# Linear attention with decay and a token-mixing layer on one core: the receptance of the last batch loaded one token to a partition and turned by DMA transposes, two decay tables made in halves, and another order of all instructions

## The chip, the cores and the metric

The program runs on one of the eight cores of one Trainium2 chip. The metric is the device time of one execution in microseconds (us). A core has a matrix engine (TensorE, PE in the profile), a vector engine (VectorE, DVE), an engine for activation functions (ScalarE, ACT), a general engine (GpSimd, POOL) and a sequencer that only issues transfers (SyncE, SP). Each engine works through its own instructions in the order in which they were written, and waits on semaphores for the others. Transfers (DMA) are issued by SP, POOL or ACT and moved by sixteen DMA engines.

## The reference

There are 4 batches of 768 tokens, 8 heads of 48 channels. All arrays are in 32-bit floats.

```python
for t in range(S):                        # attention with a decaying state, per batch and head
    cur = einsum('bhd,bhe->bhde', u * k_t, v_t)
    y[:, :, t] = einsum('bhd,bhde->bhe', r_t, state + cur)
    state = w * state + einsum('bhd,bhe->bhde', k_t, v_t)
x = y.transpose(0, 2, 1, 3).reshape(B, S, 384)
theta = x @ w_theta                       # token mixing with a phase
yr = einsum('ts,bsd->btd', w_tok_r, x * cos(theta))
yi = einsum('ts,bsd->btd', w_tok_i, x * sin(theta))
u = x + yr + yi
out = u + maximum(u @ w_ch, 0)
```

## The kernel before

**The attention in chunks.** The tokens of a batch are cut into 6 chunks of 128, and the chunks are worked on in 3 pairs (`front`, one round of its loop for each batch and pair). In a chunk the factor w^(t-s) of a score is split: k is multiplied by w^-(t+1), the table `wpinv`, into `Kw`, and r by w^t into `Rw`, both with tokens on the partitions (L457). For the scores both are needed with channels on the partitions. So `flips` transposes eight blocks of 128x128 on TensorE (L416) into a bank of PSUM, and ACT or DVE copies the bank out (L206 and L207) into `KT` or `RT`. In the last batch (`turn_k`) `KT` is made by a DMA transpose from SP instead (`turned`, L425). The scores go to two banks (L487), DVE multiplies them by the mask of earlier tokens into `mAT` (L492), and then come the parts of the output: the diagonal term (`PD` on DVE L497, `dg`, then `yd` L512), the state's update (`Ta` and `St`, L539 to L547, copied to `Sb`), the state's share (L560) and the chunk's own share (L569). DVE adds them into `x` (L583).

**How r is laid out.** `load_r` brings a pair's 256 tokens with two neighbouring tokens in one partition (128 x 8 x 96 numbers, one issue of 384 KB). So the two halves of `Rw` hold the even and the odd tokens and take two tables, `wpow[:, 0]` and `wpow[:, 1]`; the copy out of PSUM puts the tokens back into order. k and v come one token to a partition, with one issue of 192 KB for each chunk (`load`).

**The mixing layer.** `x` is transposed to `xT` (in the last batch by DMA transposes). A matmul with `Wth` gives theta (L605), ACT takes sine and cosine into `sc` (L609), DVE multiplies by `x` into `z` (L612). `mixing` runs for each batch in two halves of 384 tokens: matmuls with the token weights `WrT` and `WiT` (L641), DVE adds `xT` into `uT` (L652), a transposed copy `un` of it is made, the channel matmul follows (L685), DVE finishes a tile into `fin` (L690) and SP stores it (L695). In batch 0 a mixing part is six matmuls of 128 columns. The token weights arrive through POOL's own transfers into six buffers `stg` (L395), are transposed on TensorE (L402) and copied out.

**What sets the order.** Each operation is a task with a number; `Plan` keeps what each one reads and writes. `ORDER` is a table of all tasks in the order in which they are written: `108P2` is task 108 on TensorE with its result in bank 2, and the letters P, V, A, G, S stand for TensorE, VectorE, ScalarE, GpSimd and SyncE. `emit` goes through the table; the letter says which engine runs the task, where more than one can. One more wait is added there: where DVE and POOL both run tasks that are marked as using their common port, a POOL task waits for the marked DVE task that was written last before it:

```python
            if t.port and letter == "V":
                last = ins
            elif t.port and letter == "G" and last is not None:
                tc.add_manual_dep(ins.ins, last.ins.name, SYNC, reason="shared port")
                last = None
```

Every load and store of batch data, and every DMA transpose, is issued by SP in the order of the table. What stands behind a transpose or a store on SP goes out only when that one's data is ready.

**The start.** ACT issues the load of w (`w_row`), TensorE spreads it over the partitions with one matmul (L274), ACT takes its logarithm (L314) and makes `wpinv` and the two tables `wpow` by exponentials (L319). `Wth` is loaded by POOL (L384), after a cast (L378) that holds it back until a load of batch 0 has landed; the first `stg` buffers are held back in the same way.

Of the kernel before, what the change touches and what calls it, by code (L numbers as in the profile page):

```python
# [16 lines left out]
F32 = mybir.dt.float32  # L17
# [11 lines left out]
6G 4G 8G 10G 16G 7G 11G 13G 1V 0A 27A 26A 21S 22S 23S 79S 78S 80S 3A 5V 12G 14V 29A 28A 128S 2P0 17A 18A 36G  # L29
9G 38V 40P1 19A 85G 20A 37V 39V 41A 42P2 43A 45P34 83V 87P5 48P67 88A 30A 31A 51V 84V 47V 46V 49V 86G 33G  # L30
89P0 52P1 90A 32A 134V 126S 24S 95P24 132V 25S 53V 98V 131V 137P5 99P3 92P60 82S 127S 81S 130S 129S 50V 96V
97V 100A 44A 55P1 138A 56V 64P3 174G 34G 35G 190G 212G 186G 178G 54G 182G 94V 59V 133V 60V 58A 57A 63P7 66P
67V 65V 187G 191G 179G 91A 135P2 102P4 68P5 136A 103V 104G 61A 69A 105A 62A 106A 143P01 74P7 93V 146V 101V
111P32 114P 112P 70P6 147P5 107V 144V 115V 113V 183G 170G 171G 108G 175G 148V 139A 76A 75A 71A 109A 150P4
151V 152G 154A 153A 72A 140P02 116P7 145V 117V 216S 188P3 192P5 142V 141V 110G 118P4 122P1 149G 189A 119A
193A 120A 77V 73V 124A 155P72 156P 158P 180P6 367P0 184P3 368P 185A 123A 159V 157V 181V 172P5 160P2 215S
214S 217S 261S 218S 262S 263S 265S 310S 264S 309S 206G 209G 200G 173A 360P4 361P 176P7 121V 203G 220G 161V
125V 222V 221V 219V 15G 162P6 166P3 353P1 177A 362P 354P 363P 355P 225P2 163A 164A 168A 167A 165V 169V 223P5
369P 370P 364P 226A 227A 224V 234V 231P76 232V 228P32 365P 356P 357P 238P5 366V 233V 239V 242V 266G 268G
235P7 371P 372P 241A 229V 267G 240G 270P4 373V 230V 376P6 358P 359V 236A 207P5 246P7 249P 247P3 210P0 378P2  # L40
374P1 271A 208V 403P4 201P5 377V 211A 202A 404P 405P 406P 407P 408P 204P6 311S 312S 313S 426S 473S 213G 197G
194G 375A 269V 237V 250V 248V 379A 205A 409V 316G 396P0 272P5 414P1 251P7 397P 398P 399P 400P 401P 243V 274G
273A 252A 244A 281V 285P2 275P34 278P65 314G 402V 282P7 286V 287G 245A 283A 288A 276V 290V 415A 280V 277V
# [100 lines left out]
def kernel(  # L144
# [13 lines left out]
    nc = tc.nc  # L158
    B, H, S, D = r.shape
    HD = H * D  # L160
    C = 128
# [16 lines left out]

    def turn_k(b):
        return b >= 3  # L180

    def turn_x(b):
        return b >= 3

# [8 lines left out]
    def bank(tok):  # L193
        return bank_t[P.bank_of[tok]]
# [546 lines left out]
```

## Time and profile before

| | |
|---|---|
| median of three runs | 136.80 us (136.79 to 137.02) |
| the profiled execution | 137.21 us |
| its span from first to last instruction | 135.5 us |
| PE busy in the span | 122.2 us |
| DVE busy | 114.2 us |
| ACT busy | 78.0 us |
| POOL busy | 68.8 us |
| granted clock of TensorE | 1.00 |

The profile shows one execution. Its span leaves out 1.7 us of its own 137.21 us, which lie before the first and behind the last instruction. The profile's views are: busy times of each engine; the chain of work that ended last, followed back from the last instruction; waits and what ended them; groups of equal instructions with their mean duration; the same busy times in chosen stretches of the span; and issues of transfers with the time until they landed. The trace has two rows for TensorE, matmuls (PE) and loads of stationary weights (PEld). A busy PE is not always a PE at full speed, since a matmul's end is modelled.

### The profile page before, as it was taken

Reading aid. Unit: us, or ns where it says so; the run is one execution under the profiler, and the core shown is the slowest. Engines: PE = TensorE matmul, PEld = TensorE weight load, DVE = VectorE, ACT = ScalarE, POOL = GpSimd, SP = SyncE. Lnnn points to the kernel's source line nnn. Section 1 sums busy time; section 2 is a strip of 40 time slices with the busy share of each in tenths; the row PEclk is TensorE's granted clock in tenths of the full one; section 3 lists DMA queues with packets and bytes.
Section 4 is the critical chain, followed back from the end, with each engine's and each line's share of the span. In section 5 each row is a group of like instructions: output and inputs, shape, how many; then the busy total and the mean of one; then the engine's idle time right before and its main releaser. Section 6 shows DMA issues by size and latency. Waiting matters only on the chain.

```text
span 135.5 us, 4188 instructions
## 1 busy us (share of the span) xinstructions
PE 122.2 (90%) x1667; PEld 91.9 (68%) x1667; DVE 114.2 (84%) x231; ACT 78.0 (58%) x145; POOL 68.8 (51%) x104
## 2 busy tenths in 40 slices
PE   3358778979999999999999999999999999999990
PEld 1136665858989987977766687776566676577950
DVE  5279989798999869998999999999999997575581
ACT  3665868798836779858387339799411337240020
POOL 7324477767658456548205999755249860000000
PEclk9999999999999999999999999999999999999999
DMA  4999999999998993399999977997989439734945
GB/s 78 225 252 203 192 186 258 222 217 190 238 211 198 192 188 63 137 204 237 244 193 229 254 139 200 151 202 148 223 220 203 97 69 112 171 119 174 92 171 177
DMA packets 79781, 24.65 MB, mean 182 GB/s; under 512 B 74257, under 2 KB 79762, under 8 KB 79762
## 3 DMA queue, kind: packets, MB, share of 16 engines
q1 hardware_dynamic: 76400, 21.44, 75.4%
q0 software_dynamic: 2528, 2.95, 13.1%
q8 instruction: 13, 0.21, 0.6%
q10 hardware_dynamic: 834, 0.00, 0.3%
q14 instruction: 6, 0.05, 0.1%
HBM read 20.06 MB, written 4.72 MB: 183 GB/s over the span
## 4 chain that ended last, share of the span: by engine, by line
PE 68%; DVE 14%; DMA 8%; issue 3%; ACT 2%; SPq 1%; POOL 1%; DVEq 0%; POOLq 0%
PE bank L641 31%; PE bank L416 11%; PE bank L685 7%; PE bank L605 5%; DMA stg<-in_moe_w_tok_r_dram 5%; PE bank L487 4%; DVE mAT L492 4%; DMA ld<-in_r_dram 4%; PE bank L525 3%; PE bank L569 2%; PE bank L402 2%; PE bank L560 2%; ACT RT L206 2%; DVE z L612 1%; DVE fin L690 1%
## 5 line engine op out<-in xcount | busy, mean ns | idle before, releaser
L641 PEld LDWEIGHTS <-z 128*128 128x128 bf16 x468 | 34.3, 98 | 11.1 <-DVE z L612 0.4
L641 PE MATMUL bank<-WrT,z 128*128 128x128 bf16 (+2 forms) x234 | 31.8, 264 | 0.2 <-DVE z L612 0.2
L641 PE MATMUL bank<-WiT,z 128*128 128x128 bf16 (+2 forms) x234 | 31.8, 264 | 0.0
L492 DVE TENSOR_TENSOR mAT<-bank,mask 128x512 bf16<-128x512 f32 x48 | 31.0, 679 | 0.2 <-PE bank L487 0.2
L457 POOL TENSOR_TENSOR Kw<-ld,wpinv 128x384 bf16<-128x384 f32 x17 | 17.1, 1012 | 14.5 <-DVE yd L512 5.4
L612 DVE TENSOR_TENSOR z<-sc,x 128x768 bf16<-128x768 bf16 x24 | 14.2, 604 | 2.5 <-ACT sc L609 2.5
L605 PE MATMUL bank<-Wth,xT 128*128 128x384 bf16 x72 | 15.5, 334 | 0.9 <-DVE xT L207 0.6
L609 ACT ACTIVATE sc<-bank,pi 128x384 bf16<-128x384 f32 x24 | 13.9, 588 | 4.2 <-PE bank L605 3.5
L206 ACT ACTIVATE Sb<-St 64x192 bf16<-64x192 f32 x29 | 10.3, 358 | 9.8 <-DVE St L547 3.7
L206 ACT ACTIVATE RT<-bank 128x1024 bf16<-128x1024 bf16 x12 | 12.3, 1027 | 6.1 <-PE bank L416 6.0
L652 DVE TENSOR_TENSOR uT<-bank,xT 128x384 bf16<-128x384 f32 (+1 forms) x25 | 13.0, 534 | 2.9 <-PE bank L641 2.7
L685 PE MATMUL bank<-Wch,uT 128*128 128x384 bf16 (+2 forms) x75 | 14.7, 319 | 0.0
L512 POOL TENSOR_TENSOR yd<-dg,vb 128x768 bf16<-128x768 f32 x9 | 13.3, 1475 | 0.7 <-ACT sc L609 0.6
L547 POOL TENSOR_TENSOR St<-Ta,wC 128x192 f32<-128x192 f32 x12 | 6.7, 556 | 13.4 <-DVE Ta L541 6.2
L583 DVE TENSOR_TENSOR x<-bank,yd 128x384 bf16<-128x384 f32 x24 | 12.3, 549 | 1.4 <-POOL yd L512 0.8
L457 POOL TENSOR_TENSOR Rw<-ld,wpow 128x384 bf16<-128x384 f32 x12 | 11.9, 1002 | 2.5 <-DVE Rw L457 2.3
L609 ACT ACTIVATE sc<-bank 128x384 bf16<-128x384 f32 x24 | 11.4, 494 | 1.8 <-PE bank L605 1.8
L690 DVE SCALAR_TENSOR_TENSOR fin<-bank,un 128x384 f32<-128x384 f32 x21 | 10.8, 548 | 0.9 <-DMA un<-uT 0.7
L487 PE MATMUL bank<-RT,KT 64*128 64x128 bf16 x192 | 9.2, 235 | 2.0 <-ACT RT L206 2.0
L206 ACT ACTIVATE un<-bank 128x384 bf16<-128x384 bf16 x8 | 3.7, 484 | 11.7 <-PE bank L416 11.7
L497 DVE TENSOR_TENSOR PD<-RT,KT 128x1024 bf16<-128x1024 bf16 x12 | 8.2, 686 | 2.0 <-ACT RT L206 1.9
L206 ACT ACTIVATE KT<-bank 128x1024 bf16<-128x1024 bf16 x7 | 7.1, 1021 | 4.2 <-PE bank L416 4.2
(81 smaller groups left out, 199.6 us busy)
## 6 DMA issues: line engine op xcount, KB each, us to landing
ld<-in_k_dram SPq DMA_DIRECT2D x24, 192.0 KB, 4.6
ld<-in_r_dram SPq DMA_DIRECT2D x12, 384.0 KB, 4.8
ld<-in_v_dram SPq DMA_DIRECT2D x24, 192.0 KB, 4.7
out_dram<-fin SPq DMA_DIRECT2D x21, 192.0 KB, 2.0
stg<-in_moe_w_tok_r_dram POOLq DMA_DIRECT2D x6, 192.0 KB, 5.6
stg<-in_moe_w_tok_i_dram POOLq DMA_DIRECT2D x6, 192.0 KB, 5.5
out_dram<-stg SPq DMA_DIRECT2D x2, 192.0 KB, 1.9
Wth<-in_moe_w_theta_dram POOLq DMA_DIRECT2D x1, 288.0 KB, 5.7
```

What stands on the lines that cost most here:

```text
L206: return nc.scalar.activation(o, i, Act.Copy)
L416: nc.tensor.matmul(bank16(tok)[:, i * C:(i + 1) * C], s, ident, is_transpose=True, start=(i == 0), stop=(i == n - 1))
L457: lambda e, c=c, src=src, tab=tab, dst=dst: eng_of[e].tensor_mul(dst[:, c, :, :D], src, tab.rearrange("p (h d) -> p h d", h=H)),
L487: nc.tensor.matmul(bank(tk[hi])[:, hp * C:(hp + 1) * C], KT[q, c, hp, :], RT[q, hp, c, :], start=(hp == 0), stop=(hp == HP - 1))
L492: P.add((DVE, dve_ns(HP * C)), lambda e, hi=hi, tk=tk, mAT=mAT: nc.vector.tensor_mul(mAT[:, hi], bank(tk[hi]).rearrange("p (h t) -> p h t" ...
L512: lambda e, yd=yd, dg=dg, vb=vb: eng_of[e].tensor_mul(yd.rearrange("p a h d -> p (a h) d"), wide(dg, D), vb.rearrange("p a h d -> p (a h) ...
L605: nc.tensor.matmul(bank(th)[:, :HD], xT[:, dk, to * C:(to + 1) * C], Wth[:, dk, :], start=(dk == 0), stop=(dk == ND - 1))
L609: P.add((ACT, act_ns(HD) - 5 + 95 * (1 - ri)), lambda e, th=th, sc=sc, ri=ri: nc.scalar.activation(sc[:, ri], bank(th)[:, :HD], Act.Sin, * ...
L612: P.add((DVE, dve_ns(2 * HD, 2.0)), lambda e, sc=sc, to=to: nc.vector.tensor_mul(z[:, to], sc, bc(x[:, to], 1, 2)), rd=[("x", xi, to), ("s ...
L641: nc.tensor.matmul(bank(tm)[:, q * n * C:(q + 1) * n * C], z[:, so, ri, dk * C:(dk + 1) * C], WT[:, so, w], start=(s0 == 0 and ri == 0 and ...
L652: nc.vector.tensor_add(uT[:, dks[0]:dks[-1] + 1, w0:w1], bank(tm)[:, :len(dks) * (w1 - w0)].rearrange("p (d t) -> p d t", d=len(dks)), xT[ ...
L685: nc.tensor.matmul(bank(tf)[:, :(d1 - d0) * C], uT[:, dk, j * C:(j + 1) * C], Wch[:, dk, d0 * C:d1 * C], start=(dk == 0), stop=(dk == ND - 1))
```

## The change

**The last batch's r.** A new switch `turn_r` is true for batch 3. There r is loaded like k, one token to a partition, with two issues of 192 KB in place of one of 384 KB. It is multiplied by a new table `wpnat` (w^t with t counted within the chunk), and `RT` is made by a DMA transpose from SP (`turned`), so that three times eight transposes on TensorE and three copies out of PSUM go.

**The decay tables.** The matmul that spreads w is cut into two of 192 columns, each with its own bank and its own logarithm; `wpinv` is made in two halves of columns. `wpow` stays in two whole tables, and `wpnat` is one more exponential on ACT.

**The order.** The whole table `ORDER` is another one. Batch 0 begins with r on SP and not with k. Many tasks that can run on two engines have another engine than before: on DVE there are 4 more copies of `KT`, 2 of `RT`, 3 more of `dg`, 1 more each of `WiT` and `un`, and one fewer each of `Rw`, `St`, `xT`, `yd` and the clearing of `Sb`, and two fewer of `WrT`. ACT has 13 tasks fewer. POOL has 5 more copies of `Sb`, the clearing of `Sb`, and one more each of `yd`, `St` and `Rw`. TensorE, apart from the transposes, does the same work.

```diff
 ORDER = """
-6G 4G 8G 10G 16G 7G 11G 13G 1V 0A 27A 26A 21S 22S 23S 79S 78S 80S 3A 5V 12G 14V 29A 28A 128S 2P0 17A 18A 36G
...
+14G 13G 10G 9G 11G 5G 17G 12G 15G 7G 8G 16G 1V 0A 30A 29A 26S 24S 25S 84S 83S 82S 130S 27S 28S 132S 131S 2P0
...
+    def turn_r(b):
+        return b >= 3
+
...
+    wpnat = sb.tile([C, HD], F32, name="wpnat")
...
-        P.add((PE, 1300), lambda e: nc.tensor.matmul(bank("w")[:, :HD], ones, w_row, start=True,
-                                                     stop=True),
-              rd=["w_row", "ones"], acq=["w"], prio=-100, mode=3)
+        halves = [slice(i * (HD // 2), (i + 1) * (HD // 2)) for i in range(2)]
+        for i, q in enumerate(halves):
+            P.add((PE, 650), lambda e, i=i, q=q: nc.tensor.matmul(
+                bank("w%d" % i)[:, q], ones, w_row[:, q], start=True, stop=True),
+                rd=["w_row", "ones"], acq=["w%d" % i], prio=-100, mode=3)
...
+        for i, q in enumerate(halves):
+            P.add((ACT, 290), lambda e, i=i, q=q: nc.scalar.activation(
+                lw_f[:, q], bank("w%d" % i)[:, q], Act.Ln), rd=["tab0"], use=["w%d" % i],
+                wr=[("lw_f", i)], prio=-97.9)
...
     def small_tables():
+        P.add((ACT, 520), lambda e: nc.scalar.activation(wpnat, lw_f, Act.Exp, scale=tok_f[:, 0:1]),
+              rd=[("lw_f", 0), ("lw_f", 1), "tok_f"], wr=["wpnat"], prio=-97.65)
...
-            ir = load_r(b, pr)
+            ir = load(b, pr, r) if turn_r(b) else load_r(b, pr)
...
+                        (Ls[ir].rearrange("p (c h d) -> p c h d", c=2, h=H)[:, c], wpnat, "wpnat", Rw, kR)
+                        if turn_r(b) else
                         (Ls[ir].rearrange("p (h c d) -> p c h d", c=2, h=H)[:, c], wpow[:, c],
                          ("wpow", c), Rw, kR)):
...
+            if turn_r(b):
+                flat = RT.rearrange("p h c t -> p (h c t)")
+                RT = flat.rearrange("p (c h t) -> p h c t", c=2, h=HP)
+                turned(flat.rearrange("p (a t) -> p a t", t=C), Rw.rearrange("p a h e -> p (a h e)"),
+                       pb, [kR, kR + (0,), kR + (1,)], [kRT], 1900)
+            else:
+                flips(RT.rearrange("p h c (t j) -> p h (c t) j", j=2),
```

The order is seen best at three places. In these rows a name is followed by the number of its buffer, and `x2` stands for two such rows in a run.

First DVE in the first 15 us, before. `ld` are buffers of loaded data, `PD` is the product of `RT` and `KT`, `dg` the small diagonal.

```order
L457 TENSOR_TENSOR Kw_97<-ld_85,wpinv 128x8x48
L457 TENSOR_TENSOR Rw_94<-ld_86,wpow 128x8x48 x2
L457 TENSOR_TENSOR Kw_98<-ld_88,wpinv 128x8x48
L497 TENSOR_TENSOR PD_113<-RT_106,KT_110 128x1024
L457 TENSOR_TENSOR Rw_95<-ld_89,wpow 128x8x48
L492 TENSOR_TENSOR mAT_116<-bank_65,mask_70 128x512
L492 TENSOR_TENSOR mAT_116<-bank_64,mask_70 128x512
L492 TENSOR_TENSOR mAT_117<-bank_67,mask_70 128x512
L457 TENSOR_TENSOR Rw_96<-ld_92,wpow 128x8x48 x2
L207 COPY dg_128<-bank_62 128x16
L497 TENSOR_TENSOR PD_114<-RT_107,KT_111 128x1024
L457 TENSOR_TENSOR Kw_99<-ld_91,wpinv 128x8x48
```

The same place on DVE in the changed kernel:

```order
L469 TENSOR_TENSOR Rw_95<-ld_87,wpow 128x8x48 x2
L469 TENSOR_TENSOR Kw_98<-ld_86,wpinv 128x8x48 x2
L210 COPY KT_111<-bank_64 128x1024
L469 TENSOR_TENSOR Rw_96<-ld_90,wpow 128x8x48
L515 TENSOR_TENSOR PD_114<-RT_107,KT_111 128x1024
L469 TENSOR_TENSOR Kw_99<-ld_89,wpinv 128x8x48
L510 TENSOR_TENSOR mAT_118<-bank_67,mask_70 128x512
L510 TENSOR_TENSOR mAT_117<-bank_66,mask_70 128x512
L510 TENSOR_TENSOR mAT_117<-bank_65,mask_70 128x512
L210 COPY RT_108<-bank_61 128x1024
L210 COPY KT_112<-bank_62 128x1024
L469 TENSOR_TENSOR Kw_100<-ld_92,wpinv 128x8x48
```

What moved: r's product stands ahead of k's, and three copies out of PSUM that ACT made (`KT` twice, `RT` once) now stand on DVE among the products.

Second POOL between 11 and 21 us, before. `stg` are the buffers of the token weights, the one-column casts hold a transfer back, and `uw` is a small product for the diagonal term.

```order
L457 TENSOR_TENSOR Rw_95<-ld_89,wpow 128x8x48
L333 TENSOR_TENSOR uw<-u_75,w_74 64x4 x2
L378 CAST stg_154<-ld_91 128x1
L378 CAST Wth<-ld_87 128x1
L384 DMA Wth<-in_moe_w_theta_dram 128x3x384
L378 CAST stg_158<-ld_91 128x1
L378 CAST Wch<-ld_91 128x1
L378 CAST stg_157<-ld_91 128x1
L378 CAST stg_155<-ld_91 128x1
L512 TENSOR_TENSOR yd_131<-dg_128,vb_101 128x768
L378 CAST stg_156<-ld_91 128x1
L395 DMA stg_157<-in_moe_w_tok_r_dram 128x768
```

The same place on POOL in the changed kernel:

```order
L405 DMA stg_156<-in_moe_w_tok_r_dram 128x768
L405 DMA stg_157<-in_moe_w_tok_i_dram 128x768
L388 CAST stg_154<-ld_92 128x1
L388 CAST stg_155<-ld_92 128x1
L388 CAST Wch<-ld_92 128x1
L469 TENSOR_TENSOR Kw_100<-ld_92,wpinv 128x8x48
L210 CAST Sb_127<-St_125 64x4x48
L343 TENSOR_TENSOR uw<-u_75,w_74 64x4 x2
L394 DMA Wth<-in_moe_w_theta_dram 128x3x384
L388 CAST stg_158<-ld_92 128x1
L530 TENSOR_TENSOR yd_132<-dg_129,vb_102 128x768
L565 TENSOR_TENSOR St_126<-Ta_124,wC 128x192
```

What moved: two transfers of token weights go out ahead of `Wth`, and `Wth` stands behind a copy `Sb`, which waits for the first state that DVE computes.

Third SP in the last batch, before. `in_k`, `in_r` and `in_v` are the inputs.

```order
L425 DMA_TRANSPOSE KT_110<-Kw_98 128x8x128
L353 DMA ld_85<-in_k_dram 128x8x48
L425 DMA_TRANSPOSE un_147<-uT_144 128x9x128
L353 DMA ld_85<-in_k_dram 128x8x48
L353 DMA ld_87<-in_v_dram 128x8x48 x2
L353 DMA ld_88<-in_k_dram 128x8x48 x2
L695 DMA out_dram<-fin_150 128x384
L425 DMA_TRANSPOSE KT_111<-Kw_99 128x8x128
L695 DMA out_dram<-fin_151 128x384
L695 DMA out_dram<-fin_152 128x384
L364 DMA ld_89<-in_r_dram 128x8x96
```

The same place on SP in the changed kernel:

```order
L435 DMA_TRANSPOSE KT_111<-Kw_99 128x8x128
L713 DMA out_dram<-fin_153 128x384
L713 DMA out_dram<-fin_151 128x384
L363 DMA ld_90<-in_r_dram 128x8x48
L435 DMA_TRANSPOSE RT_108<-Rw_95 128x8x128
L363 DMA ld_90<-in_r_dram 128x8x48
L363 DMA ld_89<-in_k_dram 128x8x48
L435 DMA_TRANSPOSE KT_112<-Kw_100 128x8x128
L363 DMA ld_91<-in_v_dram 128x8x48
L435 DMA_TRANSPOSE RT_109<-Rw_96 128x8x128
L363 DMA ld_91<-in_v_dram 128x8x48
L435 DMA_TRANSPOSE KT_113<-Kw_101 128x8x128
```

What moved: the three transposes of r stand between the transposes of k, the first of them behind two stores of batch 1, and the transpose `un` of batch 1 has gone further back.

More of the change, by code (lines that the diff above doesn't have):

```diff
@@ L34 @@
[L34 to L38, printed above, removed]
@@ L71 @@
+853V 813V 803P3 839P2 840P 841P 858P4 806P1 844P0 845P 846P 836P 847P 837P 842P 777S 780S 783S 801V 802S
+823V 804V 807V 848V 859A 838V 866P6 825P7 824S 805S 808S 843V 856P3 854P4 863P1 867V 826V 855V 857A 868S
+827S 864V 860P0 828P5 831P2 869P6 861V 829V 832V 870V 865S 862S 830S 833S 871S
 """
```

101 lines of the change are left out of this document (50 added, 51 removed).

## The prediction

> **What bounds the kernel now.** I read the page's head first, then the chain of work that ended last, then the busy times in stretches cut where the chain changes its engine, and last what DVE waited for. In the rows of the chain the columns are the start and the length in us.
>
> ```profile
> span 135.5 us, 4188 instructions
> 0.81 0.45 SPq L353
> 1.93 4.85 DMA ld<-in_r_dram
> 25.19 6.39 DMA stg<-in_moe_w_tok_r_dram
> 33.47 0.97 PE bank L605 x6
> 82.07 0.19 DVE x L583
> 98.23 0.43 PE bank L525 x16
> 130.74 0.50 PE bank L685 x3
> ```
>
> The chain starts with the load of r, goes through the front of batch 0 and a transfer of token weights, and reaches the last theta of batch 0 at 33.47 + 0.97 = 34.44. Behind that it is TensorE up to 82.07, DVE up to 98.23, then TensorE up to 131.24. So two engines share the bound. The stretches below are cut where DVE has finished the last `x` of batch 0 (31.2) and the last masked score `mAT` (111.5); the numbers behind the stretch's length are the busy times of PE, PEld, DVE, ACT and POOL.
>
> ```profile
> 0.00:10.00 10.00, 4.04 (x26) 2.30 (x26) 5.00 (x16) 5.45 (x7) 4.98 (x18) 1.00 0.84 182
> 0.00:31.20 31.20, 21.91 (x290) 16.45 (x290) 24.40 (x54) 21.75 (x38) 17.96 (x43) 1.00 1.03 204
> 31.20:111.50 80.30, 79.89 (x1207) 61.01 (x1205) 75.54 (x149) 50.59 (x96) 50.25 (x62) 1.00 0.91 184
> 82.00:98.00 16.00, 16.00 (x209) 10.95 (x207) 15.95 (x32) 13.43 (x26) 9.07 (x12) 1.00 1.03 192
> 111.50:135.50 24.00, 20.38 (x176) 14.44 (x174) 14.24 (x31) 5.68 (x12) 0.63 (x1) 1.00 0.68 145
> ```
>
> DVE is idle for 31.20 - 24.40 = 6.80 us in the first stretch, 5.00 of them in the first ten, and for 80.30 - 75.54 = 4.76 us in the second. Between 82 and 98 it is idle for 0.05. TensorE is idle for 0.4 in the second stretch. Whoever shortens one of the two alone gains little. What DVE waited for longest in the second stretch (sum in us, times, longest):
>
> ```profile
> DVE PD L497 <- ACT RT L206: 1.5, 2, 1.3
> DVE x L583 <- POOL yd L512: 0.8, 2, 0.5
> ```
>
> **The prices.** Groups of equal instructions: the last number before the second bar is the mean of one in ns. The rows under the dots are pieces of the chain, and then issues of transfers with KB and median us to landing.
>
> ```profile
> L207 DVE COPY KT<-bank 128x1024 bf16<-128x1024 bf16 x2 | 1.4, 692 | 0.2 <-PE bank L416 0.2
> L206 ACT ACTIVATE RT<-bank 128x1024 bf16<-128x1024 bf16 x12 | 12.3, 1027 | 6.1 <-PE bank L416 6.0
> L492 DVE TENSOR_TENSOR mAT<-bank,mask 128x512 bf16<-128x512 f32 x48 | 31.0, 679 | 0.2 <-PE bank L487 0.2
> L207 DVE COPY WrT<-bank 128x768 bf16<-128x768 bf16 x3 | 1.6, 550 | 0.2 <-PE bank L402 0.2
> L207 DVE COPY un<-bank 128x384 bf16<-128x384 bf16 x4 | 1.4, 348 | 0.9 <-PE bank L416 0.9
> L207 DVE COPY dg<-bank 128x16 f32<-128x16 f32 x3 | 0.5, 166 | 0.0
> L512 DVE TENSOR_TENSOR yd<-dg,vb 128x768 bf16<-128x768 f32 x3 | 3.1, 1048 | 0.0
> L547 DVE TENSOR_TENSOR St<-Ta,wC 128x192 f32<-128x192 f32 x4 | 1.4, 344 | 0.0
> L457 DVE TENSOR_TENSOR Rw<-ld,wpow 128x384 bf16<-128x384 f32 x12 | 7.3, 637 | 0.5 <-DMA ld<-in_r_dram 0.4
> L690 DVE SCALAR_TENSOR_TENSOR fin<-bank,un 128x384 f32<-128x384 f32 x21 | 10.8, 548 | 0.9 <-DMA un<-uT 0.7
> L305 DVE MEMSET Sb<- 128x960 uint32 x1 | 0.9, 858 | 0.1
> ...
> 33.14 0.34 PE bank L402 x6
> 41.64 0.34 PE bank L641 x6
> 54.95 0.49 PE bank L685 x3
> 80.49 0.45 PE bank L416 x8
> ...
> ld<-in_r_dram SPq DMA_DIRECT2D x12, 384.0 KB, 4.8
> ld<-in_k_dram SPq DMA_DIRECT2D x24, 192.0 KB, 4.6
> Wth<-in_moe_w_theta_dram POOLq DMA_DIRECT2D x1, 288.0 KB, 5.7
> KT<-Kw SPq DMA_TRANSPOSE x3, 4.1
> xT<-x SPq DMA_TRANSPOSE x6, 2.4
> ```
>
> The one price that no row has is a copy of `RT` on DVE. It cannot cost less than the equal copy of `KT` (0.69) and, at the rate of the slowest copy out of PSUM, `mAT` with 512 numbers in 0.679, not more than 1.36. I take 1.03, what ACT needs for it.
>
> Three rows from the timeline (start and length in us) are needed too. The first has the two tables for r, which end at 6.03, the second the last `x` of batch 0, which ends at 31.2, and the third a product of r on DVE that took 1.55 us against the mean of 0.64 while POOL multiplied at the same time.
>
> ```profile
> 4.92 1.11 ACT L319 ACTIVATE wpow<-lw_f,tok_f 128x384 f32<-128x384 f32 x2
> 30.17 1.02 DVE L583 TENSOR_TENSOR x<-bank,yd 128x384 bf16<-128x384 f32 x2
> 33.45 1.55 DVE L457 TENSOR_TENSOR Rw<-ld,wpow 128x384 bf16<-128x384 f32 x1
> ```
>
> **The change, part by part.** *The start, up to the last `x` of batch 0.* By the two orders DVE has three more copies of `KT` there (3 x 0.69 = 2.08), one of `RT` (1.03), two of token weights (2 x 0.55 = 1.10) and one more `yd` (1.05), and goes without one `St` (0.34), one `dg` (0.17) and one `xT` (0.55, a copy of the size of `WrT`): 5.26 - 1.06 = +4.2 us. The clearing of `Sb` (0.86) goes too, but it lay in the first ten us, where DVE is half idle, and so saves nothing. From the 4.2 comes what DVE can make up: at most the 6.80 - 5.00 = 1.8 us that it idles between 10 and 31.2, and at most 1.1 because r is now issued first (at 0.81 in place of 1.93, in the chain's first rows; but both loads of k are now behind it). So the shift lies between 1.3 and 4.2; I take 2.8, the middle. In this shift lies the later `Wth`: it now stands behind the copy of the first state on POOL and lands 5.7 us after its issue, but the theta that needs it is later by about the shift as well.
>
> *The second stretch, up to the last `mAT`.* DVE gets one `KT` (0.69), one `RT` (1.03), four `dg` (0.66), one `un` (0.35), and loses one `Rw` (0.64), three `WrT` (1.65), two `yd` (2.10) and three `fin` (1.64), which now stand behind it: 2.73 - 6.03 = -3.3 us. DVE's idle 4.76 us can shrink: ACT has 13 tasks fewer, and 1.5 us were waits for its `RT`. They can grow: POOL has five more copies of `Sb` and one more each of `yd`, `St` and `Rw`, and 0.8 us were waits for its `yd`; and three `PD` now wait for DMA transposes. Bounds -2 and +2; I take +0.3, a little on POOL's side, since a product on DVE beside one on POOL is slow (the row of 1.55 us).
>
> *Behind the last `mAT`* TensorE has two more channel tiles than before (2 x 0.49 = +1.0). The three more `fin` of DVE lie beside it, where DVE is busy for 14.24 of 24 us.
>
> The sum over DVE: 2.8 - 3.3 + 0.3 + 1.0 = +0.8 us.
>
> *The same over TensorE.* From the last theta of batch 0 on it starts 2.8 us later and has less to do: 24 transposes are gone (3 x 0.45 = 1.35), two token-weight blocks (0.68) and five mixing parts of batch 0 (1.70) stand ahead of that theta now: 2.8 - 3.73 = -0.9 us. That is 1.7 us earlier than DVE allows, so DVE's sum decides, and what was taken from TensorE becomes a wait for DVE.
>
> *Costed at nothing.* The halves of the tables: the tables' exponentials ended at 6.03 and r landed at 1.93 + 4.85 = 6.78, so the first products waited for loads; without that cover they are worth 0.4 at most. The extra exponential and ACT's 13 tasks: ACT idles 9.4 us in the first stretch. The split loads of r: two of 192 KB need about the time of one of 384 KB each (4.6 and 4.8), six issues on SP in place of three, early enough. The waits of SP: the first transpose of r stands behind two stores that need DVE's `fin` of batch 1; the scores that want it come some ten mixing parts later on TensorE (10 x 0.49), which is about what issue and landing take (4.1 plus half a us); if DVE is late there, scores and so `PD` are late.
>
> **The forecast.** The profiled execution's own time is 137.21 us, 1.7 more than its span and 0.4 above the median. The sum is a difference between two spans, and I carry it to the median unchanged: 136.8 + 0.8 = 137.6 us, slower. With the bounds of the shift and of the idle time narrowed to their middle halves it lies between 137.1 and 138.8.
>
> **Rivals.** *DVE catches up, and it is faster.* The place is DVE's idle time, 1.8 us in the start and 4.76 in the second stretch. If the shift is 2.0 and the idle time shrinks by 1.0 (most of the waits for ACT's `RT`), the sum over DVE is 2.0 - 3.3 - 1.0 + 1.0 = -1.3, TensorE's is 2.0 - 3.73 = -1.7, and the time is 135.5. At the best of both bounds TensorE decides with 1.3 - 3.73 = -2.4: 134.4. It turns where DVE makes up 1.1 us more than I gave it. For it speaks that ACT, which DVE waited for longest, has less to do; against it that DVE has no idle time between 82 and 98 to give.
>
> *Nothing to measure.* The two sums may meet between: 136.8. A difference within 0.2% of the time (0.27 us) is about what measurements of this kernel cannot tell from none.
>
> *The transposes of r come late.* A DMA transpose of eight blocks landed 4.1 us after issue, one of three blocks 2.4, so 0.8 a block; if eight cost eight times that, 6.4, each `RT` lands 2.3 later. TensorE's matmuls stand in a fixed order, so the first scores of the last batch wait for it once, and the later pairs' transposes queue behind one another on SP: 137.6 + 2 = 139.6. For it speaks that DMA engines are as busy as 1.03 and 0.91 of their time in the two long stretches, and that the transposes of k go through the same queue; against it the 4.1 itself, measured in that stretch.
>
> A rule speaks for this rival: the Trainium skill, page "VectorE: DVE Perf Modes", section "The three transpose paths", gives 1309 ns for a 128x128 block by DMA and 390 ns on TensorE, and advises TensorE where the result may go to PSUM. By it eight blocks would take 10.5 us (an estimate) and the time would be above 141. The trace does not agree for eight blocks in one transfer: 4.1 us.
>
> **How the numbers follow.** The forecast gets 0.40, the faster rival 0.35, no difference 0.10, late transposes 0.15. So faster has 0.35, same 0.10, slower 0.40 + 0.15 = 0.55. The range runs from 135.2, which leaves out the best fifth of the faster case, to 139.2, which leaves out the worst half of the late transposes.
>
> **What would show it.** Right: the last `x` of batch 0 ends near 34, 2 to 4 us later than 31.2; TensorE shows waits for DVE in the middle; DVE is over 96% busy from there to its last `mAT`, which ends near 111.3, and TensorE ends about 20.9 us behind it. Wrong: an early end of that stretch (before 109.5) means that DVE caught up; scores that wait for `RT<-Rw` mean late transposes; a copy of `RT` on DVE near 0.7 or 1.3 moves the sum by 0.6 down or up; and a start that ends before 33 makes it faster.

## The result, and the profile after

The changed kernel takes 138.15 us (median, 137.75 to 139.24), the kernel before beside it on the same chip 136.80 (136.59 to 137.02). The ratio is 1.0107, with a 95% interval of 1.0066 to 1.0148: slower, as forecast. The forecast was 137.6 us with a range from 135.2 to 139.2. The profiled execution took 138.46 us. Its span of 136.7 us stands against 135.5 before, 1.2 more. The ratios here and below leave out executions more than 1.5% above the fastest of their kernel; the profile of turn_late shows one of these, so it has no landmarks in the table below.

The page's head, and pieces of the chain of work that ended last (start and length in us):

```profile
span 136.7 us, 4146 instructions
18.74 5.89 DMA Wth<-in_moe_w_theta_dram
24.77 1.12 PE bank L623 x3
35.80 1.34 PE bank L659 x24
94.15 2.44 PE bank L659 x15
100.90 1.44 POOL yd L530
102.84 0.47 DVE x L601
103.32 4.64 DMA RT<-Rw
108.00 0.62 PE bank L505 x16
114.10 4.02 DMA xT<-x
130.73 0.50 PE bank L703 x3
```

Before, the chain ran through r's load and a load of token weights to the last theta of batch 0. Now it reaches the first theta (L623, at 24.77) through the load of `Wth`. From about 30 to 100 nearly all long pieces are TensorE's. In the last batch a transfer of `RT`, another of `xT`, and POOL's `yd` are on it, which were not there before.

The same stretches as before, cut at the end of the last `x` of batch 0 (35.03) and of the last `mAT` (111.3); behind the length stand the busy times of PE, PEld, DVE, ACT and POOL:

```profile
0.00:10.00 10.00, 5.07 (x40) 3.72 (x40) 5.26 (x19) 5.37 (x9) 6.69 (x18) 1.00 0.91 187
0.00:35.03 35.03, 25.61 (x330) 19.97 (x331) 26.90 (x57) 21.16 (x39) 22.62 (x50) 1.00 1.07 206
35.03:111.30 76.27, 76.00 (x1140) 57.12 (x1137) 72.34 (x148) 42.70 (x82) 52.16 (x63) 1.00 0.86 181
111.30:136.70 25.40, 21.32 (x181) 14.83 (x179) 15.51 (x33) 5.85 (x13) 0.00 (x0) 1.00 0.67 176
```

Against the prediction's rows the start is 35.03 - 31.20 = 3.8 us longer, the second stretch 80.30 - 76.27 = 4.0 shorter, and what lies behind the last `mAT` 25.40 - 24.00 = 1.4 longer: +1.2 in all. DVE's busy time grew by 26.90 - 24.40 = 2.5 us in the start and fell by 75.54 - 72.34 = 3.2 in the second stretch. Its idle time grew from 6.80 to 8.13 and fell from 4.76 to 3.93. TensorE stands still for 0.27 us of the second stretch.

Prices that the prediction had to estimate (groups and issues), and waits that are new or longer (sum in us, times, longest):

```profile
L210 DVE COPY RT<-bank 128x1024 bf16<-128x1024 bf16 x2 | 2.4, 1224 | 0.3 <-PE bank L426 0.2
RT<-Rw SPq DMA_TRANSPOSE x3, 4.0
PE bank L623 <- DMA Wth<-in_moe_w_theta_dram: 0.9, 1, 0.9
PE bank L505 <- DMA RT<-Rw: 0.2, 1, 0.2
DVE WrT L210 <- PE bank L412: 1.1, 1, 1.1
DVE Ta L559 <- PE bank L543: 1.0, 1, 1.0
DVE x L601 <- POOL Rw L469: 0.9, 1, 0.9
```

### The profile page after: what moved, and what is told of

Same layout as the page of the kernel before. It is cut to its first block, busy times and chain, and to the rows that moved or that the text cites. A ratio compares the mean times of both kernels' runs of the same rounds, so it can differ in the third digit from the quotient of the medians.

```text
span 136.7 us, 4146 instructions
## 1 busy us (share of the span) xinstructions
PE 122.9 (90%) x1645; PEld 91.9 (67%) x1645; DVE 114.8 (84%) x235; ACT 69.7 (51%) x132; POOL 74.8 (55%) x113
## 4 chain that ended last, share of the span: by engine, by line
PE 66%; DMA 11%; DVE 7%; POOL 7%; ACT 3%; issue 3%; DVEq 0%; SPq 0%; POOLq 0%; ACTq 0%
PE bank L659 29%; PE bank L426 10%; PE bank L623 9%; PE bank L703 5%; DMA Wth<-in_moe_w_theta_dram 4%; DMA RT<-Rw 3%; PE bank L505 3%; DMA xT<-x 3%; ACT sc L627 3%; PE bank L587 3%; PE bank L578 2%; PE bank L543 2%; PE bank L412 2%; POOL Rw L469 1%; DVE Rw L469 1%
## 5 line engine op out<-in xcount | busy, mean ns | idle before, releaser
L659 PEld LDWEIGHTS <-z 128*128 128x128 bf16 x468 | 34.3, 98 | 11.0 <-issue 0.7
L659 PE MATMUL bank<-WiT,z 128*128 128x128 bf16 (+2 forms) x234 | 31.2, 264 | 0.0
L530 POOL TENSOR_TENSOR yd<-dg,vb 128x768 bf16<-128x768 f32 x10 | 14.8, 1476 | 4.2 <-DVE z L630 2.7
L623 PE MATMUL bank<-Wth,xT 128*128 128x384 bf16 x72 | 15.5, 340 | 1.6 <-DMA Wth<-in_moe_w_theta_dram 0.9
L627 ACT ACTIVATE sc<-bank,pi 128x384 bf16<-128x384 f32 x24 | 13.3, 580 | 6.3 <-PE bank L623 6.1
L630 DVE TENSOR_TENSOR z<-sc,x 128x768 bf16<-128x768 bf16 x24 | 13.0, 567 | 3.2 <-ACT sc L627 3.1
L209 ACT ACTIVATE Sb<-St 64x192 bf16<-64x192 f32 x24 | 8.6, 359 | 7.8 <-DVE St L557 4.8
L469 POOL TENSOR_TENSOR Rw<-ld,wpow 128x384 bf16<-128x384 f32 x8 | 7.9, 995 | 8.5 <-DVE Kw L469 2.7
L209 ACT ACTIVATE vb<-ld 128x768 bf16<-128x768 f32 x10 | 8.4, 840 | 5.8 <-DMA ld<-in_v_dram 5.8
L426 PE MATMUL bank<-ident,Rw 128*128 128x128 bf16 x72 | 7.1, 248 | 3.6 <-POOL ident masks.py:199 1.8
L209 ACT ACTIVATE RT<-bank 128x1024 bf16<-128x1024 bf16 x7 | 7.2, 1026 | 5.3 <-PE bank L426 5.1
L623 PEld LDWEIGHTS <-xT 128*128 128x128 bf16 x72 | 6.1, 99 | 5.2 <-ACT Sb L209 1.0
```

Source lines behind the costliest of these rows:

```text
L209: return nc.scalar.activation(o, i, Act.Copy)
L426: nc.tensor.matmul(bank16(tok)[:, i * C:(i + 1) * C], s, ident, is_transpose=True, start=(i == 0), stop=(i == n - 1))
L469: lambda e, c=c, src=src, tab=tab, dst=dst: eng_of[e].tensor_mul(dst[:, c, :, :D], src, tab.rearrange("p (h d) -> p h d", h=H)),
L530: lambda e, yd=yd, dg=dg, vb=vb: eng_of[e].tensor_mul(yd.rearrange("p a h d -> p (a h) d"), wide(dg, D), vb.rearrange("p a h d -> p (a h) ...
L623: nc.tensor.matmul(bank(th)[:, :HD], xT[:, dk, to * C:(to + 1) * C], Wth[:, dk, :], start=(dk == 0), stop=(dk == ND - 1))
L627: P.add((ACT, act_ns(HD) - 5 + 95 * (1 - ri)), lambda e, th=th, sc=sc, ri=ri: nc.scalar.activation(sc[:, ri], bank(th)[:, :HD], Act.Sin, * ...
```

## The experiments

Four theories are told apart. P is the prediction: DVE's sum decides. T says that from about 33 us on TensorE's own queue decides, so that only its waits count, above all those for `Wth` and for `RT`. H came from the traces: TensorE works at half rate in the start, and the changed order puts off its full rate. C, which came last, is a chain in the last batch through POOL and SP. The expectations compare with the changed kernel's 138.15 us or its ratio.

All runs with their landmarks, from the same three cuts of each profile (us):

| run | ratio to before, 95% interval | first theta starts | last `x` of batch 0 ends | last `mAT` ends | span |
|---|---|---|---|---|---|
| before | 1 | 22.4 | 31.2 | 111.5 | 135.5 |
| changed | 1.0107 (1.0066 to 1.0148) | 24.8 | 35.0 | 111.3 | 136.7 |
| after_again | 1.0084 (1.0053 to 1.0115) | 24.8 | 35.1 | 111.0 | 136.1 |
| wth_early | 1.0230 (1.0193 to 1.0266) | 26.5 | 36.3 | 112.5 | 137.6 |
| copies_act | 1.0269 (1.0240 to 1.0298) | 27.2 | 37.2 | 113.1 | 138.2 |
| spin_gap | 1.0106 (1.0067 to 1.0145) | 24.9 | 34.4 | 110.8 | 136.2 |
| spin_after | 1.0108 (1.0067 to 1.0149) | 25.0 | 34.3 | 111.3 | 136.5 |
| spin_before | 1.0006 (0.9976 to 1.0036) | 24.3 | 32.5 | 112.5 | 136.3 |
| rw_early | 1.0204 (1.0161 to 1.0247) | 24.8 | 35.1 | 112.3 | 137.4 |
| rw_first | 1.0156 (1.0124 to 1.0189) | 24.4 | 34.2 | 111.7 | 136.8 |
| rw_dve | 1.0112 (1.0058 to 1.0165) | 24.2 | 34.3 | 111.0 | 136.3 |
| r_on_pe | 1.0475 (1.0443 to 1.0507) | 24.7 | 35.1 | 115.6 | 141.0 |
| turn_before | 1.0667 (1.0632 to 1.0703) | 22.5 | 31.3 | 120.4 | 144.3 |
| turn_late | 1.0938 (1.0889 to 1.0987) | - | - | - | - |

The landmarks of a row are those of one profiled execution, the ratio is of all. The profiled execution of spin_before took 138.03 us, against a median of 136.83. And rw_early, rw_first, rw_dve and r_on_pe change only the last batch, so that their start is that of the changed kernel. The last `x` of batch 0 ends between 34.2 and 35.1 in these profiles, so differences of up to 0.9 us at this mark arise without an edit there.

Two columns can be read before any experiment is told. From the last `mAT` to the end of the span it is 25.0 to 25.5 us in every run of the changed order, and 23.8 to 24.0 in every run of the order before. And a later start arrives at the last `mAT` nearly in full: wth_early +1.3 and +1.2, copies_act +2.1 and +1.8.

**The start: the load of `Wth`.**

```diff
 ORDER
-194G 38G 182G 183G 187G ... 37G 39G 190G
+194G 38G 39G 182G 183G 187G ... 37G 190G
```

> The changed kernel with one move: POOL issues the load of Wth right behind the cast that holds it back, ahead of the copy of the first state and of five other casts. In the changed kernel it was issued at 18.74 and TensorE waited 0.9 us for it at the first theta. Theory P (the prediction: DVE's sum decides, the later Wth lies inside DVE's shift): no difference to the changed kernel, 138.1 us, 1.0 to 1.4 above the kernel before. Theory T (TensorE's own queue decides from about 33 us on, and the wait for Wth is one of the places where it lost what the missing transposes gave): 0.5 to 0.9 less than the changed kernel, about 137.4, and the first theta starts near 23.5 in place of 24.77.

It became slower, 139.7 us, which neither theory expected. TensorE no longer waits for `Wth`, but for the first token weights, which now load behind it, and longer:

```profile
PE bank L411 <- DMA stg<-in_moe_w_tok_r_dram: 2.8, 1, 2.8
0.00:36.26 36.26, 24.85 (x330) 19.45 (x331) 26.05 (x57) 21.07 (x39) 22.30 (x50) 0.91 1.07 205
```

The DMA engines are taken for 1.07 of the time in this start as in the changed kernel's, so a transfer put ahead pushes another back. TensorE's matmuls stand in a fixed order, and in the changed order the flips of token weights stand ahead of the first theta. Moving these flips as well, the other half of this experiment, wasn't tried.

**The start: DVE's copies.**

```diff
 ORDER
-45V ... 92V ... 94V ... 140V
+45A ... 92A ... 94A ... 140A
```

> The changed kernel with four copies in the start given back to ACT: the three KT and the one RT of batch 0 that it had put on DVE. DVE has 3 x 0.69 + 1.2 = 3.3 us less work before the last x of batch 0, ACT four copies of 1.03 more. Theory P (DVE's load in the start is what made it slower): the last x of batch 0 ends 1.3 to 2.8 earlier than 35.0 and the time falls until TensorE's sum decides, 1.0 to 1.7 less than the changed kernel: 136.4 to 137.1. Theory T (TensorE decides and only waits for the first copies to be ready): a copy takes 1.03 on ACT and 0.69 on DVE, so the scores of batch 0 start later, 0 to 1.5 us more than the changed kernel: 138.1 to 139.6.

It became slower by more than any theory expected: 140.1 us, where T ended at 139.6 and P forecast a gain. This is the run against the prediction's way of sizing the start:

```profile
0.00:37.16 37.16, 25.88 (x330) 20.38 (x331) 24.51 (x53) 24.17 (x43) 22.02 (x50) 1.00 1.05 200
37.16:113.07 75.91, 75.63 (x1140) 57.09 (x1137) 72.33 (x147) 42.97 (x82) 52.07 (x63) 1.00 0.90 180
PE bank L504 <- ACT RT L208: 2.0, 1, 2.0
PE bank L504 <- ACT KT L208: 1.1, 1, 1.1
```

DVE has 26.90 - 24.51 = 2.4 us less to do, and the start is 2.1 us longer. The scores wait for the copies on ACT instead. How long the start takes is here not set by DVE's sum, but by how soon each piece is ready.

**The start: TensorE's rate.** Six transposes of `x` took 0.85 us at 22.45 and 0.51 at 28.54 in the changed kernel. By the gaps between matmuls the full rate comes at 24.4 us in the kernel before, at 27.3 in the changed kernel's first profile and at 28.7 in that of after_again. The following runs fill TensorE's gaps with matmuls that nobody reads: spin_gap the one ahead of the first theta, spin_after (whose edit is shown) and spin_before nearly all of the start, so that it works almost without a break.

```diff
+    wfill = sb.tile([C, C], BF16, name="wfill")
...
+    for i, n in enumerate([17, 8, 3, 24, 14, 8, 9, 5, 5, 18, 9, 13, 4, 4, 5, 5, 4, 6, 20, 6, 4, 11]):
+        def spin(e, i=i, n=n):
+            for _ in range(n):
+                nc.tensor.matmul(bank(("spin", i))[:, :C], wfill, wfill, start=True, stop=True)
+        P.add((PE, 56 * n), spin, rd=["wfill"], acq=[("spin", i)])
```

> The changed kernel once more, beside the kernel before on this chip, so that the three others stand against it. All theories: 1.0 to 2.0% above the kernel before (first measured: 1.0107 with 1.0066 to 1.0148).

The changed kernel once more: 138.05 us, 1.0084.

> The changed kernel with eight matmuls of 128 columns that nobody reads, put on TensorE ahead of the first theta, where it waited for Wth from 23.85 to 24.77 (8 x 0.107 = 0.86 us at the rate of that stretch). Theory H (half rate: TensorE takes 1.03 us for eight transposes until 27.3 us and 0.45 from then on, in the kernel before until 24.4; it goes to the full rate only after a stretch of unbroken work, and the wait for Wth broke it; a microsecond at half rate costs 0.47): the full rate comes between 23 and 26, and the time is 0.5 to 1.5 us less than the changed kernel's on the same chip. Theory T (the waits themselves are the cost, not the rate): no difference, since the wait is only filled. Theory P (DVE's sum): no difference.

> The changed kernel with 202 matmuls of 128 columns that nobody reads, put on TensorE into the gaps from 3.7 to 30.5 us (17 ahead of the first transposes of r, then 3 to 24 in each gap). Theory H (TensorE runs at half rate until it has worked for a stretch without a break): the full rate comes near 8 to 12 in place of 27.3, eight transposes of batch 0 take 0.45 in place of 1.03, and the time is 1.5 to 3 us less than the changed kernel's on the same chip, below the kernel before. Theories T and P: the matmuls only stand in the way of real work: no gain, 0 to 2 us more.

> The same for the kernel before: 204 matmuls of 128 columns that nobody reads, in the gaps of TensorE from 3.4 to 30.2 us. Theory H: the full rate comes near 8 to 12 in place of 24.4, and the time is 0.7 to 2 us less than the kernel before. Against the changed kernel with the same filling: if the later full rate was what took back the 24 transposes (1.35 us) in the start, the changed kernel is now the faster by about 0.4 us, 1.35 less the 0.95 us that it waits in the last batch. Theories T and P: no gain, 0 to 2 us more, and the changed kernel stays 1.0 to 1.5 us behind.

The filling did to the rate what it should. In spin_gap the first theta already runs at the full rate, its three matmuls in 0.65 us, and yet the time is the changed kernel's (1.0106). Eight transposes of `Kw`, in the changed kernel and in spin_after:

```profile
12.20 1.03 PE L426 MATMUL bank<-ident,Kw 128*128 128x128 bf16 x8 [0.35 <-POOL Kw L469]
```

```profile
12.57 0.61 PE L428 MATMUL bank<-ident,Kw 128*128 128x128 bf16 x8
0.00:34.34 34.34, 31.51 (x532) 28.03 (x533) 26.24 (x58) 21.06 (x39) 22.53 (x50) 1.00 1.08 208
34.34:111.26 76.92, 76.38 (x1140) 57.12 (x1137) 72.44 (x148) 42.45 (x82) 52.08 (x63) 1.00 0.89 179
```

TensorE is at its full rate 17 us earlier, and the time is that of the changed kernel: 1.0108 against 1.0084 and 1.0107. The last `x` of batch 0 ends 0.7 us earlier than in the changed kernel, and the second stretch takes that much longer. The kernel before with the same filling is at 1.0006, so the changed kernel stays as far behind as without it.

For those 0.7 us no filling is needed. In rw_first and rw_dve, whose start is the changed kernel's, the first theta (at 24.44 and 24.24) runs at the full rate as well. The first row is the changed kernel's, the second rw_first's:

```profile
24.77 1.12 PE L623 MATMUL bank<-Wth,xT 128*128 128x384 bf16 x3 [0.92 <-DMA Wth<-in_moe_w_theta_dram]
24.44 0.65 PE L622 MATMUL bank<-Wth,xT 128*128 128x384 bf16 x3 [0.66 <-DMA Wth<-in_moe_w_theta_dram]
```

Their last `x` of batch 0 ends at 34.2 and 34.3. In after_again, rw_early and r_on_pe, where the first theta takes 1.12 us, it ends at 35.1. So when the full rate comes differs between executions of one order, and a late one goes with 0.7 to 0.9 us at this mark. Of that little or nothing is left at the last `mAT`: 110.8 in spin_gap and 111.3 in spin_after, against 111.3 and 111.0. Theory H falls as the cause of the longer time.

**The last batch: the late `RT`.** On POOL the last product of r ended at 103.3, its transpose landed at 107.96, and TensorE's scores started at 108.00. Three runs move that product.

```diff
 ORDER, rw_early
-645G 725G
+725G 645G
 ORDER, rw_first
-698G 724G 722G 723G 644A 645G 725G ... 726S 727S
+723G 725G 698G 724G 722G 644A 645G ... 727S 726S
 ORDER, rw_dve
-793V ... 698G 724G 722G 723G 644A 645G 725G
+698G 724G 722G 723G 725V 793V ... 644A 645G
```

> The changed kernel with one move: on POOL the last product of r (second half of the last pair) goes ahead of the yd of the last batch's first pair. It then ends near 101.9 in place of 103.3, and the third DMA transpose of r can be issued and land 1.4 us earlier, near 106.6 in place of 107.96. Theory P (DVE's sum decides): yd is 1.0 us later, DVE's x behind it too, so 0 to 1.0 us more than the changed kernel: 138.1 to 139.1. Theory T (TensorE decides, and the third late RT starts three waits of TensorE with 0.94 us in sum, at 108.0, 118.2 and 119.9): 0.5 to 0.9 less than the changed kernel, about 137.4.

> The changed kernel with both products of r of the last pair moved on POOL ahead of a state update and the two products of k, into time in which POOL waited (94.9 to 97.5), and the third DMA transpose of r ahead of that of k on SP. yd keeps its place. RT should land near 103 in place of 107.96, KT near 106. Theory T: the three waits of TensorE in the last batch (0.94 us in sum in the changed kernel's profile) go: 0.5 to 0.9 us less than the changed kernel (1.0084 to 1.0107 of the kernel before), that is 1.002 to 1.006. Theory P (DVE's sum decides): no difference to the changed kernel. If the state update, later by 0.5 us, is what x waits for, it is slower.

> The changed kernel with the last product of r moved from POOL to DVE, ahead of four additions to uT at 99.9 us; POOL's other products keep their order. RT of the last pair can be issued near 101.5 and land near 105.7 in place of 107.96, yd keeps its place on POOL or is a little earlier, and DVE has one product more (0.55 us) ahead of x. Theory C (in the last batch a chain through POOL and SP decides: products of r, then yd, and the transpose of r behind them; what was moved on POOL alone only put yd in the place of RT): 0.4 to 0.9 us less than the changed kernel, that is 1.003 to 1.008 of the kernel before. Theory P (DVE decides): 0.3 to 0.6 us more than the changed kernel, 1.011 to 1.014.

In rw_early `yd` comes a microsecond later and DVE's `x`, which stands ahead of `PD` and the masks on DVE, waits for it. In rw_first it is the same, since the product went into POOL's queue ahead of `yd` all the same. The first row is rw_early's, the second rw_first's:

```profile
DVE x L600 <- POOL yd L529: 1.4, 2, 1.2
35.12:112.25 77.13, 76.52 (x1140) 56.98 (x1137) 73.00 (x148) 42.56 (x82) 51.89 (x63) 1.00 0.87 176
```

```profile
DVE x L600 <- POOL yd L529: 1.4, 2, 1.2
34.17:111.67 77.50, 76.79 (x1144) 57.24 (x1141) 73.48 (x147) 42.67 (x81) 51.76 (x63) 1.00 0.87 179
```

The second stretch is 0.9 and 1.2 us longer than the changed kernel's 76.27; rw_first's start ended 0.9 earlier, so that at its last `mAT` 0.4 is left of the 1.2. Only rw_dve moves the product without delaying `yd`. There the transpose goes out at 100.89 in place of 103.32, and TensorE shows no wait for `RT` any more:

```profile
100.89 1.25 SPq L434 DMA_TRANSPOSE RT<-Rw  x1
34.29:111.00 76.71, 76.51 (x1146) 57.33 (x1143) 72.88 (x148) 42.58 (x82) 51.51 (x62) 1.00 0.88 180
111.00:136.30 25.30, 21.41 (x181) 14.81 (x179) 15.51 (x33) 5.88 (x13) 0.00 (x0) 0.99 0.65 172
```

The time is 1.0112, the changed kernel's. The last `mAT` ends at 111.0, as in after_again. DVE works from 97 to 111 with masks, r's product, additions to `uT`, `x`, `PD` and masks, and once more `x`, `PD` and masks, idle for 0.5 us of it, and an `RT` that is there earlier finds it busy:

```profile
97.00:111.00 14.00, 13.92 (x182) 8.91 (x180) 13.54 (x26) 2.01 (x7) 10.58 (x13) 1.00 0.65 135
```

TensorE is as full: 13.92 us here, 13.77 in the changed kernel. The scores that need the third `RT` start at 107.44 in place of 108.00, but in after_again, the same kernel as the changed one, they start at 107.66. So the late transpose is seen on TensorE, and removing its wait gives no gain in the profile. T's and C's forecast (C: 1.003 to 1.008) isn't borne out, though the interval, 1.0058 to 1.0165, does not exclude its upper end. Nor can P's rise of 0.3 to 0.6 us be told from none, with 1.0112 against 1.0107 and 1.0084.

**The turning on TensorE again.**

```diff
-                turned(flat.rearrange("p (a t) -> p a t", t=C), Rw.rearrange("p a h e -> p (a h e)"),
-                       pb, [kR, kR + (0,), kR + (1,)], [kRT], 1900)
+                flips(flat.rearrange("p (a t) -> p a t", t=C),
+                      [Rw[:, c, 2 * hp:2 * hp + 2, :] for c in range(2) for hp in range(HP)],
+                      ("TR", b, pr), pb, [kR, kR + (0,), kR + (1,)], [kRT])
```

> The changed kernel with the last batch's r still loaded one token to a partition, but turned on TensorE (24 transposes of 128x128, three copies out of PSUM on ACT) and not by DMA. Theory P (DVE decides, TensorE has 1.7 us to spare): no difference to the changed kernel, 138.1 us. Theory T (TensorE decides; the DMA transposes saved it 24 x 0.056 = 1.35 us and cost it 0.94 us of waits in the last batch): 0.4 more than the changed kernel, about 138.5. If the late transposes cost more than they save, it is faster than the changed kernel: below 137.7.

It is 3.7% behind the changed kernel, more than any theory had, because of where the flips went. The third flips got a bank that DVE's masks still read, and a copy of `RT` on ACT stood ahead of the `dg` that `yd` waits for:

```profile
PE bank L425 <- DVE mAT L510: 1.5, 1, 1.5
PE bank L543 <- ACT dg L208: 0.6, 1, 0.6
35.06:115.64 80.58, 77.79 (x1164) 58.26 (x1161) 72.41 (x148) 45.24 (x85) 52.14 (x63) 1.00 0.80 159
```

TensorE's work in the stretch grew by 1.8 us (76.00 to 77.79), its idle time by 2.5. The run doesn't separate the price of the transposes from that of their place. Whether another of the eight banks was free when the third `RT` was wanted, it doesn't show.

**The turning alone, in the order before.** 24 transposes and three copies go, the loads of r are split and `wpnat` is made. In turn_late each DMA transpose stands where the flips stood. In turn_before the third pair's load, products and transpose are moved ahead.

```diff
 ORDER, both (numbers of the kernel before)
-629P4 630A ... 675P5 676A ... 722P1 723A
+629S ... 675S ... 722S
 ORDER, turn_before in addition: load 714S and its second half ahead of 668S, products 718G 720G ahead of 719G, 722S behind 674S
```

> The kernel before, in its own order, with the turning of r alone: r of the last batch loaded one token to a partition (two issues of 192 KB), multiplied by the table wpnat, RT by DMA transposes, 24 transposes on TensorE and three copies on ACT left out. The transposes of the first two pairs stand where the TensorE transposes stood; for the third pair the load of r, its two products on POOL and the DMA transpose are moved ahead, behind the KT transpose of the second pair, so that RT should land near 103, well ahead of its scores at 108.5. Theory T (from about 33 us on TensorE's queue decides): what leaves TensorE leaves the time, 24 x 0.056 = 1.35 us, less up to 0.4 for waits: 135.4 to 135.9, 0.990 to 0.993 of the kernel before. Theory P (between 82 and 98 DVE decides, as the chain of the kernel before said, and DVE's work is unchanged): the saving becomes waits for DVE: 136.5 to 137.0.

> The same turning of r in the kernel before, but with nothing moved ahead: the third pair's products on POOL end at 105.8 as before, so its DMA transpose lands 4 to 4.6 us later, near 110, where the scores stood at 108.5. Theory T with late transposes: TensorE saves 1.35 us and waits some 1.5 us for RT, and the last x, xT and theta are later by as much: 136.8 to 138.3, 1 to 2.5 us more than with the products moved ahead. Theory P: DVE waits for the late PD and scores just as long, since it has no other work there: 137.5 to 138.5. If a transpose that lands late costs nothing, it is the same as with the products moved ahead.

Both are far slower. In turn_before nothing is lost until the first transpose of r; then SP stands still. Its row of loads ends at 79, and its next instruction starts at 86.84:

```profile
74.81 4.18 SPq L358 DMA_DIRECT2D ld<-in_v_dram  x4
86.84 1.33 SPq L430 DMA_TRANSPOSE RT<-Rw  x1
...
SPq L430 <- POOL Rw L464: 7.8, 1, 7.8
...
PE bank L500 <- DMA KT<-Kw: 5.2, 1, 5.2
...
31.30:86.00 54.70, 54.65 (x887) 44.07 (x884) 50.80 (x101) 37.63 (x69) 34.34 (x43) 1.00 0.85 176
86.00:96.00 10.00, 4.56 (x66) 3.15 (x66) 5.39 (x11) 5.12 (x12) 3.79 (x4) 0.92 0.87 183
```

The transpose waited 7.8 us for POOL's product of r. Behind it on SP stood two loads of r, three stores and the transpose of `KT`, and TensorE then waited 5.2 us for `KT`. In the kernel before, the flips of this pair ran on TensorE at 87.19, also right behind POOL's product, but nothing on SP queued behind them. So the turning can't be had in the old order by putting each transpose where its flips were. A version with the transposes behind those loads wasn't tried. turn_late is about 4 us slower still, where 1 to 2.5 were expected, for the same reason once more: in its trace the third pair's loads of r go out on SP at 105.58, its transpose waits another 5.9 us for POOL's product and goes out at 112.69, in turn_before at 108.24.

No run beats the kernel before. And none has the changed order with the turning placed well on TensorE, or the order before with the turning placed well on SP, so what the turning and the order each cost is not separated.

## Why the prediction was right, point by point

**The sum.** It was +2.8 in the start, -3.0 in the second stretch, +1.0 behind it: +0.8. The profiles show +3.8, -4.0 and +1.4: +1.2, and the medians +1.35. Slower was right, and the last `mAT` at 111.3 was right to the tenth, but that is partly luck: two terms were off by 1.0 in opposite directions, and part of both is one piece of work on the other side of the mark. TensorE's busy time up to the end of the last theta of batch 0, before and then changed:

```profile
0.00:34.44 34.44, 24.93 (x329) 18.91 (x330) 27.25 (x58) 24.58 (x42) 20.54 (x47) 1.00 1.04 202
0.00:38.11 38.11, 28.69 (x373) 22.66 (x374) 29.98 (x62) 22.57 (x41) 23.61 (x51) 1.00 1.05 203
```

That theta is 3.7 us later with 3.8 us more work ahead of it, and TensorE's idle time is the same, 9.5 and 9.4. Of this work 2.4 us are the token-weight blocks and mixing parts that the prediction counted there (0.68 + 1.70). The narrower range of 137.1 to 138.8 does not follow from the bounds that the prediction names: their middle halves (2.0 to 3.5, and -1 to 1) give 135.5 to 139.0.

**The start.** The shift was mis-sized: 3.8 for 2.8 (3.0 to 3.9 in the profiles with the same start), within the bounds of 1.3 to 4.2. Its working failed, not only its size. DVE's busy time grew by 2.5, not by 4.2, mainly since the clearing of `Sb` (0.86) did leave it, and the two `yd` took 0.95 each where the one before took 1.25. And DVE made up nothing: its idle time between 10 us and the cut rose by 1.6 (8.13 - 4.74 = 3.4, from 1.8), in waits for TensorE's flips and state products (1.1 and 1.0) and for ACT's `sc` (0.8). That copies_act made the start longer with less work on DVE shows that a sum of DVE's work was the wrong measure there. `Wth`, costed at nothing, was 0.9 us of wait on TensorE ahead of the first theta; wth_early shows that it can't be had back by itself. The later full rate goes with 0.7 to 0.9 of the shift, and DVE's copies are excluded. The rest stays open: the supply of transfers is only suggested by wth_early, and there is a rival that no run tested. The first `x` of batch 0 is already 1.8 us late (19.47 to 21.25). POOL makes `uw` at 18.33 there and not at 12.13, behind the copy `Sb` that waits for the first state; TensorE's product with it, `dg` and `yd` (at 19.75, before 17.30) come behind, and `x` waits for that `yd`.

**The second stretch.** DVE's work fell by 3.2 (forecast 3.3). Its idle time fell by 0.8, where +0.3 was taken, within the bounds of -2 and +2. The waits for ACT's `RT` went, and POOL's extra work showed little: `x` waited 1.2 us for POOL (0.9 put down to a product of r, 0.3 to `yd`), against 0.8 before.

**Behind the last `mAT`.** +1.4 for +1.0: TensorE's matmuls end 1.2 later against that mark, the rest is DVE and the last store. All runs of the one order and all of the other agree on this term to 0.5 us, the firmest of the sum. No run moved the two tiles back.

**TensorE's saving becomes waits for DVE.** This step was wrong. TensorE stands still for 0.27 us of the second stretch. The saving was used up earlier: its last theta of batch 0 starts 3.7 us later (34.1 to 37.8) and its work in the second stretch is 79.89 - 76.00 = 3.9 less, so with the start as it was TensorE's sum and DVE's meet. Which of the two decides in the middle can't be told from these runs, nor in the last batch, where rw_dve has both of them full.

**Smaller terms.** A copy of `RT` on DVE takes 1.22 us (taken 1.03, bounds 0.69 to 1.36). DVE's share from the start to its last `mAT` is 72.34 / 76.27 = 95%, not over 96. The first transpose of r went out at 90.98 and landed at 95.0, ahead of its scores at 96.5, so the wait behind the stores was covered, as costed. The third made TensorE wait, but rw_dve, without that wait, was no faster. The halves of the tables were put at nothing because the first products waited for loads. That holds for r, but the first product of k (on POOL at 5.10) waited 1.6 us for `wpinv`. With r first, the first flips start at 5.64 in place of 6.15.

**The rivals.** That DVE catches up was half right: it did in the second stretch, by 0.8, and the start, where it idled 1.6 more, took that back. Late transposes are not the cause: eight blocks landed in 3.6 to 4.6 us, median 4.0, as the trace of before had it for k. By the Trainium skill, page "VectorE: DVE Perf Modes", section "The three transpose paths", it would have been 10.5 (the estimate of the prediction); the measurement decides.

## What to carry to other kernels

Work taken off an engine does not pay by itself, if the order that comes with it costs more elsewhere: here 24 transposes went (1.35 us), and with a start longer by 3.8 us and two more tiles behind the last mask the kernel became slower. In a start that waits for transfers and for one piece after another, count when each piece is ready, not how much one engine has to do. A DMA transpose needs a place in its queue where its source is already there, since all loads behind it wait with it.

## What was not expected of the hardware

**Half rate on TensorE, which the granted clock doesn't show.** For the first 24 to 31 us of the runs without filling eight transposes take 1.03 us, later 0.61, and the granted clock is 1.00 all along. In wth_early TensorE reached the full rate at about 17.5, stood still for 2.8 us, and was at half rate again until 27.5; there the clock's column (the third from the end) does show it:

```profile
20.00:24.00 4.00, 2.62 (x42) 2.23 (x42) 1.11 (x3) 1.86 (x4) 2.95 (x6) 0.60 1.10 226
24.00:28.00 4.00, 3.65 (x49) 2.67 (x44) 2.45 (x7) 1.86 (x5) 0.84 (x2) 0.54 1.18 212
```

The Trainium skill, page "TensorE: Matmul & The Clock Gate", section "What you observe", gives gaps of 107 and 56 ns for matmuls of 128 columns before and after some 4 us of sustained work. The traces agree on the gaps (in the chain of before eight transposes at 19.36 take 0.85 us, 0.106 each, and six at 33.14 take 0.34, 0.057 each), and spin_after, busy from 3.7 us on, had the full rate by 10. With short gaps in the work it took 24 to 31 us. Yet earlier full rate brought no shorter time here.

**A copy that spreads its output costs DVE more than ACT.** The copy of `RT`, which puts neighbouring tokens back side by side, takes DVE 1.22 us, the equal-sized copy of `KT` 0.68; ACT takes 1.03 for `RT`.
